# Loading the first row of wq in two halves, from two engines' DMA queues

## The chip, the cores and the metric

The kernel runs on one core of a Trainium2 chip. A core has five engines with an instruction stream each: TensorE (PE; PEld is its loading of weights), VectorE (DVE), ScalarE (ACT), GpSimd (POOL) and SyncE (SP, which here only issues DMAs). They are tied together by semaphores. Sixteen DMA engines move data between HBM and the core's memory of 128 partitions; SyncE and ScalarE each have a DMA queue that feeds them. The metric is device time in microseconds: the kernel before takes 99.17 us (median of three runs, 99.14 to 99.19).

## What is computed

One token passes through attention over a sliding window of a cached sequence and, in parallel, an MLP; both get the normalised input and their sum is added to x. All tensors are bf16.

```python
# x (1,1,1024), 32 query heads, 4 key/value heads, head size 128, window W = 4096 of Sk = 65536
xn = layernorm(x)
q = (xn @ wq).reshape(1, 1, 32, 128).transpose(0, 2, 1, 3)            # wq (1024, 4096)
k = repeat(k_cache[:, :, Sk - W:, :], 8, axis=1)                       # v alike
p = softmax(einsum("bhqd,bhkd->bhqk", q, k) * 128 ** -0.5)
attn = einsum("bhqk,bhkd->bhqd", p, v).transpose(0, 2, 1, 3).reshape(1, 1, 4096) @ wo
y = layernorm(xn)
mlp = gelu(y @ w1 + b1) @ w2 + b2                                      # w1 (1024, 3584)
return x + attn + mlp
```

With one token every weight is used once: 39.9 MB are read, and the arithmetic is matrix times vector.

## The kernel before

Nothing is tiled over the output; each weight matrix is loaded whole, in one or a few large DMAs, and its rows are spread over the partitions. For wq, partition p holds rows 8p to 8p+7, and "row r" of the loaded matrix below means the r-th of these eight in every partition (4096 bf16, 8 KB a partition, 1 MB in all). `WQ_CHUNKS = [1, 7]` loads row 0 by one DMA and rows 1 to 7 by a second, each with a semaphore of its own (`s_wq[0]`, `s_wq[1]`).

SyncE issues all the large loads in one order: wq's row 0, wq's rows 1 to 7 (57 KB a partition), then, after a wait for GpSimd's constants (L210), the K window, w1 and the V window; w2 once the product with wq is done (L323, for it overwrites wq); wo in chunks of 16, 8, 4 and 3 rows and two half rows, once the product with w1 is done (L422). ScalarE issues three small ones from its own queue: x (L191) and b1 (L192), which both come after a wait for two GpSimd memsets (L190, it counts POOL's `b1z`), and b2 (L246).

The work around these loads, in order: VectorE waits for x (`dve.wait_ge(s_x, 16)`, L241) and transposes it (L242); a chain of short instructions on VectorE, GpSimd, TensorE and ScalarE (L248 to L278) makes the two layer norms, `XNTb` for the attention and `YTb` for the MLP. TensorE multiplies `XNTb` with wq (`wide_product`, L306 to L319, recorded at L283): it waits for `s_wq[0]`, does the eight matmuls of row 0, waits for `s_wq[1]`, and does the 56 of rows 1 to 7. VectorE, ScalarE and TensorE bring q into the shape `QB` (L327 to L350). VectorE then waits for K and transposes it in place in four steps (L355); TensorE multiplies the scores behind each step; a softmax follows (L375 to L405). Then TensorE multiplies w1 (L411 to L418), p with V (L470 to L476), w2 (L516) and, chunk by chunk as it lands, wo (L545 to L551, after each chunk a few matmuls of `keep_busy` on no data of use). The last three rows of wo and the addition of the two half sums come at L556 to L583, and SyncE stores the result (L585).

On each engine the order is as written in the code; the wait that counts is a semaphore's value. A DMA adds 16 to its semaphore when it has landed:

```python
act.wait_ge(POOL.sem, C["b1z"])
act.dma_start(XB4[0:128:32, :], x_rows).then_inc(s_x, 16)
act.dma_start(B1R[0:128:32, :], b1_rows).then_inc(s_b1, 16)
```

Of the kernel before, what the change touches and what calls it, by code (L numbers as in the profile page):

```python
# [20 lines left out]
NQ = 4096  # L21
# [5 lines left out]
WQ_CHUNKS = [1, 7]  # L27
# [24 lines left out]
def bass_parallel_sum__sliding_block_cached__mixer_channel_mlp__decode_kernel(  # L52
# [18 lines left out]
    pe, dve, act, pool, sp = nc.tensor, nc.vector, nc.scalar, nc.gpsimd, nc.sync  # L71

    def sems(name, n):
        return [nc.alloc_semaphore(f"{name}{i}") for i in range(n)]

    s_x, s_b1, s_b2, s_out = (nc.alloc_semaphore(n) for n in ("s_x", "s_b1", "s_b2", "s_out"))
    s_wq = sems("s_wq", len(WQ_CHUNKS))
# [11 lines left out]
    def sb(name, shape, d):  # L89
        return nc.alloc_sbuf_tensor(name, shape, d)  # L90

    f32, bf16 = dt.float32, dt.bfloat16
    WA = sb("WA", [128, KC * NQ], bf16)
# [61 lines left out]
    wq_p = A_wq.rearrange("(p r) n -> p r n", r=KC)  # L155
# [8 lines left out]
    def load_rows(dst, src, chunks, width, semaphores, first=0, c0=0, off=0):  # L164
        for j, n in enumerate(chunks):
            sp.dma_start(  # L166
                dst[:, off + c0 * width: off + (c0 + n) * width].rearrange("p (c n) -> p c n", c=n),
                src[:, first + c0: first + c0 + n, :],
            ).then_inc(semaphores[j], 16)
            c0 += n  # L170
# [1 line left out]
    def load_cache(dst, src, sem):  # L172
        sp.dma_start(dst[:, :], src[0, :, SK - W:SK, :].rearrange("g (m b) d -> m g (b d)", m=32)).then_inc(sem, 16)

    load_rows(WA, wq_p, WQ_CHUNKS, NQ, s_wq)
    def d(ins):
        return DVE.mark(ins)

# [103 lines left out]
    def held(out, rhs, w, pos, size, start, stop, load=False):  # L282
        return pe.add_instruction(mybir.InstMatmult(  # L283
            name=nc.get_next_instruction_name(), engine=PEE, ldweights=load,
            start_tensor_calc=start, stop_tensor_calc=stop, tile_size=size, tile_position=pos,
            ins=[pe.lower_ap(rhs), pe.lower_ap(w, for_matmul_weights=True)], outs=[pe.lower_ap(out)]))
# [18 lines left out]

    def wide_product(weights, chunks, width, semaphores, vec, n, banks, name):  # L306
        for j, (k0, k1) in enumerate(chunks):
            pe.wait_ge(semaphores[j], 16)
            for k in range(k0, k1):
                w = vec[:, k:k + 1].to_broadcast([128, 32])  # L310
                for a in range(4):
                    pe.ldweights(w, tile_position=(0, 32 * a))  # L312
                for b in range(2):
                    for a in range(4):
                        lo = k * width + (2 * a + b) * n
                        last = held(PS[32 * a:32 * a + 32, banks[b] * 512: banks[b] * 512 + n], weights[:, lo:lo + n], w,
                                    (0, 32 * a), (128, 32), k == 0, k == KC - 1)
        C[name] = PE.mark(last)

    hinted = pe.mark_branch_hint_location()  # L320
    wide_product(WA, [(0, 1), (1, 8)], NQ, s_wq, XNTb, 512, [4, 5], "q")

    sp.wait_ge(PE.sem, C["q"])  # L323
# [293 lines left out]
```

## Time and profile before

| | |
|---|---|
| median of three runs | 99.17 us |
| the profiled execution | 99.34 us, of which 98.0 us are the span |
| busy: PE, DVE, ACT, POOL | 53.2, 41.8, 11.2, 8.2 us |
| read from HBM | 39.86 MB, 407 GB/s over the span |
| SyncE's queue, share of 16 DMA engines | 95.0% |
| wq row 0: issue to landing | 5.0 us |
| wq rows 1 to 7: issue to landing | 21.5 us |
| K: issue to landing | 25.9 us |

The span runs from the first to the last instruction of the execution that was profiled; the rest of its time lies around it. In the views, a line such as `22.72 5.80 PE L283 MATMUL ... [7.37 <-DMA WA<-in_A_wq_dram]` gives the start, the time to the end of the group, the engine, the line of the kernel, the operation with its tiles, and in brackets the idle time of that engine before it and what ended it. A tile is named without its number (KT is K's, later wo's; WA is wq's, later w2's; XB is x's). An engine's name with a q behind it (SPq, ACTq) is its sequencer issuing something. Windows give, for each stretch of time, the busy time of each engine with its number of instructions, the clock granted to TensorE, and the share and GB/s of the DMA engines; packets are counted in the stretch in which they start, so that short stretches can show more than 100%.

### The profile page before, as it was taken

The numbers are of one execution on the slowest core, as the hardware profiler recorded it, in microseconds if no ns is written. First come the engines' busy times: TensorE is split into PE (matmuls) and PEld (weight loads), VectorE is DVE, ScalarE is ACT, GpSimd is POOL, SyncE is SP. The second block draws the span as 40 slices with busy tenths as digits, with TensorE's granted clock in tenths as the row PEclk, the third lists the DMA queues.
The fourth block names the chain that finished last, engine by engine and source line by source line (L and its number), as shares of the span: only waits on it lengthen the run. The fifth ranks groups of instructions, "written<-read, shape, count | busy, mean of one in ns | idle before, by whom it ended". The sixth has DMA issues, their size and how long they took to land.

```text
span 98.0 us, 911 instructions
## 1 busy us (share of the span) xinstructions
PE 53.2 (54%) x376; PEld 13.4 (14%) x217; DVE 41.8 (43%) x45; ACT 11.2 (11%) x21; POOL 8.2 (8%) x33
## 2 busy tenths in 40 slices
PE   0000232007960947195361489878998677883781
PEld 0000220001100001011010111113332111220130
DVE  0000321000028899999999500987943400110042
ACT  0000527000022000000000489000000000000020
POOL 6776201000000000000000000000000000000000
PEclk9999999999999589957999755899999999999999
DMA  3999888999999988899599998889994999999960
GB/s 53 488 613 398 377 374 375 398 538 441 428 428 578 398 374 374 374 398 702 237 428 428 428 588 374 374 374 398 702 398 214 428 428 428 421 428 408 421 251 1
DMA packets 1765, 39.87 MB, mean 407 GB/s; under 512 B 216, under 2 KB 484, under 8 KB 612
## 3 DMA queue, kind: packets, MB, share of 16 engines
q1 hardware_dynamic: 1740, 39.85, 95.0%
q10 hardware_dynamic: 24, 0.01, 0.0%
q14 instruction: 1, 0.01, 0.0%
HBM read 39.86 MB, written 0.00 MB: 407 GB/s over the span
## 4 chain that ended last, share of the span: by engine, by line
DMA 52%; DVE 24%; PE 11%; POOL 5%; issue 3%; SPq 1%; ACT 1%; POOLq 0%; DVEq 0%
DMA KT<-in_A_k_cache_dram 26%; DMA KT<-in_A_wo_dram 26%; DVE KT L355 18%; PE PS L292 9%; DVE MX L375 2%; DVE MX L377 2%; POOL F L206 1%; POOL B1R L188 1%; SPq L166 1%; DVE KT L554 1%; DVE MR L388 1%; PE PS L559 1%; ACT Q L381 1%; POOL QB L198 1%; PE PS L283 1%
## 5 line engine op out<-in xcount | busy, mean ns | idle before, releaser
L355 DVE STREAM_TRANSPOSE KT<-KT 128x4096 bf16<-128x4096 bf16 x4 | 17.4, 4413 | 0.5 <-DMA KT<-in_A_k_cache_dram 0.5
L283 PE MATMUL PS<-KT,QB 128*128 128x512 bf16 x32 | 8.9, 427 | 7.6 <-DVE KT L355 7.6
L283 PE MATMUL PS<-WA,XNTb 128*32 128x512 bf16 x64 | 6.8, 605 | 7.4 <-DMA WA<-in_A_wq_dram 7.4
L292 PE MATMUL PS<-W,YTb 128*32 x64 | 8.2, 464 | 1.3 <-issue 0.9
L292 PE MATMUL PS<-V,WA 128*128 (+1 forms) x31 | 7.9, 381 | 0.5 <-issue 0.2
L292 PE MATMUL PS<-WA,GT 128*32 x56 | 6.7, 381 | 2.6 <-issue 1.8
L253 PE MATMUL PS<-XT,onesf 128*128 128x16 f32 x2 | 0.6, 385 | 10.9 <-POOL XT L251 10.9
L327 DVE CAST Q<-PS 128x512 bf16<-128x512 f32 x1 | 0.7, 691 | 12.6 <-PE PS L283 12.6
L242 DVE STREAM_TRANSPOSE XT<-XB 128x256 bf16<-128x256 bf16 x1 | 0.6, 625 | 9.7 <-DMA XB<-in_A_x_dram 9.7
L406 DVE STREAM_TRANSPOSE WA<-WA 128x4096 bf16<-128x4096 bf16 x1 | 4.4, 4436 | 0.0
L292 PE MATMUL PS<-W,OT 128*32 128x512 bf16 x48 | 2.9, 380 | 2.1 <-DMA W<-in_A_wo_dram 1.5
L367 PEld LDWEIGHTS <-QB 128*128 128x128 bf16 x16 | 1.7, 104 | 17.3 <-DVE KT L355 13.5
L554 DVE COPY KT<-PS 128x512 f32<-128x512 f32 x1 | 0.7, 692 | 7.6 <-PE PS L292 7.6
L520 DVE TENSOR_TENSOR OD<-PS,D 128x128 f32<-128x128 f32 x1 | 0.3, 292 | 8.4 <-PE PS L518 8.4
L292 PEld LDWEIGHTS PS<-V,WA 128*128 (+1 forms) x32 | 3.1, 96 | 4.7 <-issue 3.0
L283 PE MATMUL PS<-MRow,ML 128*128 128x512 bf16 x8 | 3.3, 581 | 0.7 <-DVE QB L348 0.7
L402 ACT ACTIVATE WA<-PS,NMB 128x1024 bf16<-128x1024 f32 (+1 forms) x2 | 3.1, 1536 | 1.2 <-DVE NMB L397 1.2
L381 ACT ACTIVATE Q<-PS 128x512 f32<-128x512 f32 x1 | 0.6, 597 | 22.5 <-DVE MX L377 22.5
L555 ACT ACTIVATE KT<-PS 128x512 f32<-128x512 f32 x1 | 0.6, 597 | 22.2 <-PE PS L292 22.2
L312 PEld LDWEIGHTS <-XNTb 128*32 128x32 bf16 x32 | 1.2, 138 | 12.1 <-DMA WA<-in_A_wq_dram 8.3
L292 PEld LDWEIGHTS PS<-W,YTb 128*32 x32 | 1.6, 98 | 7.5 <-issue 7.1
L257 ACT ACT_TABLE_LOAD x1 | 1.3, 1283 | 10.9 <-POOL XT L251 10.9
(105 smaller groups left out, 47.4 us busy)
## 6 DMA issues: line engine op xcount, KB each, us to landing
WA<-in_A_wq_dram SPq DMA_DIRECT2D x1, 7168.0 KB, 21.5
W<-in_B_w_dram SPq DMA_DIRECT2D x1, 7168.0 KB, 42.2
WA<-in_B_w_dram SPq DMA_DIRECT2D x1, 7168.0 KB, 47.4
KT<-in_A_k_cache_dram SPq DMA_DIRECT2D x1, 4096.0 KB, 25.9
V<-in_A_v_cache_dram SPq DMA_DIRECT2D x1, 4096.0 KB, 51.3
W<-in_A_wo_dram SPq DMA_DIRECT2D x1, 4096.0 KB, 18.9
W<-in_A_wo_dram SPq DMA_DIRECT2D x1, 2048.0 KB, 23.4
WA<-in_A_wq_dram SPq DMA_DIRECT2D x1, 1024.0 KB, 5.0
```

The lines of the kernel that those rows point to most:

```text
L257: C["std1"] = ACT.mark(act.activation(out=msx[:, 6:7], in_=msx[:, 5:6], func=ACTF.Sqrt, scale=-1.0, bias=EPSC[:, 0:1]))
L283: return pe.add_instruction(mybir.InstMatmult(name=nc.get_next_instruction_name(), engine=PEE, ldweights=load, start_tensor_calc=start, st ...
L292: return pe.add_instruction(mybir.InstMatmult(name=nc.get_next_instruction_name(), engine=PEE, ldweights=load, start_tensor_calc=start, st ...
L312: pe.ldweights(w, tile_position=(0, 32 * a))
L355: C["kt"].append(d(dve.transpose(KT[:, j * W:(j + 1) * W], KT[:, j * W:(j + 1) * W])))
L367: pe.ldweights(w, tile_position=(0, 0))
L375: d(dve.tensor_reduce(out=MX[:, 0:1], in_=PS[:, 0:2048], axis=AX.X, op=ALU.max))
L377: C["mx1"] = d(dve.tensor_reduce(out=MX[:, 1:2], in_=PS[:, 2048:4096], axis=AX.X, op=ALU.max))
L381: C["s7"] = ACT.mark(act.activation(out=S7, in_=bank(7), func=ACTF.Copy))
L402: C[f"exp{j}"] = C["exp"] = ACT.mark(act.activation(out=PT[:, lo:lo + n], in_=src, func=ACTF.Exp, bias=NMB[:, 0:1], scale=SCALE, accum_out ...
L406: C["PT"] = d(dve.transpose(PT, PT))
L554: C["S0"] = d(dve.tensor_copy(S[:, 0:DH2], bank(SB)))
```

## The change

Row 0 of wq is loaded by two DMAs of 64 partitions each, 0.5 MB apiece. SyncE issues the one for partitions 0 to 63, where it issued the whole row. ScalarE issues the one for partitions 64 to 127; it stands before every other instruction of ScalarE, and so before the wait at L190 and the loads of x and b1. Both add to `s_wq[0]`, and TensorE waits for 32 on it instead of 16. Rows 1 to 7 are loaded by SyncE as before, right after its half of row 0.

```diff
-    load_rows(WA, wq_p, WQ_CHUNKS, NQ, s_wq)
+    half_row = WQ_CHUNKS[0] * NQ
+    for eng, lo in ((sp, 0), (act, 64)):
+        eng.dma_start(WA[lo:lo + 64, 0:half_row], wq_p[lo:lo + 64, 0, :]).then_inc(s_wq[0], 16)
+    load_rows(WA, wq_p, WQ_CHUNKS[1:], NQ, s_wq[1:], first=WQ_CHUNKS[0], off=WQ_CHUNKS[0] * NQ)
     def d(ins):
         return DVE.mark(ins)
...
     def wide_product(weights, chunks, width, semaphores, vec, n, banks, name):
         for j, (k0, k1) in enumerate(chunks):
-            pe.wait_ge(semaphores[j], 16)
+            pe.wait_ge(semaphores[j], 16 if j else 32)
             for k in range(k0, k1):
```

## The prediction

> **What bounds the kernel now.** I read the chain of work that ended last first, then the order of time up to the first use of K, then fine windows of the loads, then the end of TensorE's order of time. All times are of one profiled execution: span 98.0 us, 99.34 us with the 1.34 us around it. That is 0.17 us above the median of the runs shown, 99.17, so a sum made on it loses 0.17 at the end.
>
> ```profile
> DMA 52%; DVE 24%; PE 11%; POOL 5%; issue 3%; SPq 1%; ACT 1%; POOLq 0%; DVEq 0%
> DMA KT<-in_A_k_cache_dram 26%; DMA KT<-in_A_wo_dram 26%; DVE KT L355 18%; PE PS L292 9%; DVE MX L375 2%; DVE MX L377 2%; POOL F L206 1%; POOL B1R L188 1%; SPq L166 1%; DVE KT L554 1%; DVE MR L388 1%; PE PS L559 1%; ACT Q L381 1%; POOL QB L198 1%; PE PS L283 1%
> ```
>
> Two loads make half of the chain: K, and the last rows of wo. Both are the tail of one stream, so the question is whether that stream ever pauses. In these windows the last two columns are the busy share of the 16 DMA engines and GB/s, and a packet counts where it starts:
>
> ```profile
> 6.80:7.00 0.20, 0.00 (x0) 0.00 (x0) 0.00 (x0) 0.00 (x0) 0.17 (x1) 1.00 2.66 1152
> 7.00:7.20 0.20, 0.00 (x0) 0.00 (x0) 0.00 (x0) 0.00 (x0) 0.20 (x1) 1.00 6.64 2872
> 7.20:7.40 0.20, 0.00 (x0) 0.00 (x0) 0.00 (x0) 0.00 (x0) 0.14 (x2) 1.00 0.66 287
> ...
> 9.20:9.40 0.20, 0.00 (x0) 0.00 (x0) 0.00 (x0) 0.00 (x0) 0.12 (x2) 1.00 3.97 1720
> 9.40:9.60 0.20, 0.00 (x0) 0.00 (x0) 0.00 (x0) 0.00 (x0) 0.16 (x1) 1.00 0.00 0
> 9.60:9.80 0.20, 0.00 (x0) 0.00 (x0) 0.14 (x1) 0.00 (x0) 0.00 (x0) 1.00 0.66 287
> ```
>
> 287 GB/s over 0.2 us is 57 KB: one packet, the seven rows of wq that one partition gets (7 x 8 KB). Its share, 0.66 of 16 engines over 0.2 us, is 2.11 us of one engine. So each engine starts such a packet every 2.11 us, with no gap, and one engine starts each round on its own, some 0.3 us after the rest (9.60; by the packet records 0.27 behind the next and 0.47 behind the middle one). It has that lag from its first packet of the first row (8 KB, 1126 ns; a later 8 KB packet takes 309 ns) and keeps it to the end: its first-row mark is at 5.38 us, that of the last load at 95.19. The loads are a rigid block; its start, and the latest engine in it, set the last landing.
>
> The second question is how the two DMA queues share an engine (packets, MB, share; first from 2.00 to 6.85 us, then 6.85 to 7.20):
>
> ```profile
> q1 hardware_dynamic: 150, 1.88, 93.8%
> ...
> q1 hardware_dynamic: 14, 0.80, 529.5%
> q10 hardware_dynamic: 4, 0.00, 1.9%
> ```
>
> q1 is SyncE's, q10 ScalarE's. ScalarE's load of x (4 rows of 512 B, one to an engine) is issued from 1.98 to 3.05, yet no packet of it runs before 6.85. It starts at 6.91 to 7.13, when its four engines have ended their first 57 KB packet; its completion mark comes one more such packet later, at 9.05 to 9.27; b1 one more later, at 11.17. So in this stretch the engine alternates: one packet of q1, one of q10, and each packet of q10, even a mark, costs 2.11 us.
>
> The order of time shows what waits for x:
>
> ```profile
> 0.74 0.86 SPq L166 DMA_DIRECT2D WA<-in_A_wq_dram  x2
> 1.98 1.07 ACTq L191 DMA_DIRECT2D XB<-in_A_x_dram  x1
> 9.66 0.62 DVE L242 STREAM_TRANSPOSE XT<-XB 128x256 bf16<-128x256 bf16 x1 [9.66 <-DMA XB<-in_A_x_dram]
> 14.31 1.03 PE L283 MATMUL PS<-WA,XNTb 128*32 128x512 bf16 x8
> 22.72 5.80 PE L283 MATMUL PS<-WA,XNTb 128*32 128x512 bf16 x56 [7.37 <-DMA WA<-in_A_wq_dram]
> 31.34 0.59 DVE L348 CAST QB<-PS 32x128 bf16<-32x128 f32 x2 [0.33 <-PE PS L339]
> 32.39 17.42 DVE L355 STREAM_TRANSPOSE KT<-KT 128x4096 bf16<-128x4096 bf16 x4 [0.45 <-DMA KT<-in_A_k_cache_dram]
> ```
>
> The first row's eight matmuls end at 15.34, and TensorE then waits 7.37 us for the other seven rows. Behind that, VectorE waits 0.45 us for K. So x may be 7.37 + 0.45 = 7.82 us late before the work from 32.39 on moves. The last reserve is at the end:
>
> ```profile
> 88.02 1.12 PE L298 MATMUL PS<-identf 128*128 128x512 f32 x2
> 90.63 1.04 PE L292 MATMUL PS<-W,OT 128*32 128x512 bf16 x16 [1.49 <-DMA W<-in_A_wo_dram]
> 91.60 0.81 PE L298 MATMUL PS<-identf 128*128 128x320 f32 x2
> 93.12 0.60 PE L292 MATMUL PS<-KT,OT 128*32 128x512 bf16 x8 [0.71 <-DMA KT<-in_A_wo_dram]
> ```
>
> TensorE waits 1.49 us for wo's second chunk and 0.71 us for the third: 2.20 us more.
>
> **The change, part by part.** *Issue on SyncE.* Its first DMA shrinks from 128 rows to 64; two issues stay (0.86 us for both), so the seven-row load is issued no later. Its packets can be there about 1.0 us after an issue starts (0.74 to the first packet at 1.75), by 2.7 at worst; an engine needs at least 3 x 0.31 us after its first packet's end (2.55 to 3.24) for its half of the row. No gap, price 0.
>
> *Issue on ScalarE.* One DMA more ahead of x's. SyncE's first issue took about 0.4 us, ScalarE's first 1.07. From 0.7 it ends at 1.1 to 1.8, before ScalarE's wait on GpSimd's memset is over (1.96), so x is issued when it was. If x's 1.07 was a first-use cost, it moves to the new DMA. Price on the sequencer 0. The b2 load and the rest of ScalarE's work come behind x in any case.
>
> *The stream.* The bytes of each engine stay: 4 + 4 packets of 8 KB in place of 8, and one mark more (9 ns). Changing queue costs nothing visible: an engine ends a 57 KB packet, runs x's in 27 ns, and starts the next at once. Price of the stream 0.01 us, if the half loads run at 309 ns a packet; the bounds are below.
>
> *TensorE's wait* asks for 32 in place of 16: the same wait on both halves. Behind it on TensorE stands the whole of q; ScalarE and VectorE wait for q at 28.57, SyncE too, to issue w2, whose turn comes only after v (landed at 59).
>
> *The queue that x is moved back in.* This is the step with a price. Ahead of x, in q10, each engine now has four 8 KB packets and a mark. SyncE's ring holds only four such packets before the 57 KB ones, so it is past them at 3.5 to 3.8 on x's engines. Packets of q10 that run while SyncE's 8 KB ones do are free; each that comes later costs one 57 KB packet. How many is not shown; the bounds are two rounds ahead of x's mark, as now (x at 9.66), and eight. The nearest row is x itself: queued 1.0 us before SyncE's last 8 KB packets ended at 4.8 if its delay is like that of SyncE's first load, it was still passed over until a 57 KB packet had run. If ScalarE's half does as x did, it misses SyncE's 8 KB packets and one 57 KB packet: 57 KB packets then stand ahead of its four packets, its mark, x and x's mark, seven. I take seven. x's mark then comes at 3.65 + 7 x 2.11 + 4 x 0.31 = 19.7 in place of 9.2, 10.5 us late. Then: 10.5 - 7.37 (wait for the seven rows) = 3.1 late for q; - 0.45 (wait for K) = 2.7 late from 32.39 on. From there to 88 I find no wait that absorbs it: VectorE, TensorE and ScalarE hand over within 0.1 us, and wo's issue, now at 69.5, is still before w2's last packets end at 75.5. - 1.49 = 1.2 late at wo's second chunk, - 0.71 = 0.5 at the third. The first row itself has landed by then (its last packets at about 13 and mark at 15).
>
> *Sum:* 0 + 0 + 0.01 + 0.47 = 0.5 us: 99.34 + 0.5 = 99.8, less 0.17: 99.65. With six rounds x is 8.4 late, 0.6 after VectorE's wait, and the 1.49 hides it: 99.2. With eight it is 12.6 late and 2.6 at the end: 101.7.
>
> **The rivals.** *Hidden.* The halves alternate from the start, or six rounds at most: x is late, nothing else is. For it: 10.0 us of reserve in all. Against it: x's own six microseconds of waiting. 99.2.
>
> *Faster: the start.* The end hangs on one engine's first packet (1126 ns, the others 307 to 1024). SyncE's loop reaches its 16 engines from 1.75 to 2.32; with half the rows it may reach the late ones sooner, and a second queue may fill a slow engine's start. It decides if that engine's lag goes and x is under 10 us late: 0.27 if only the next one is left (98.9), 0.47 if all are as the middle one (98.7). Against it: first packets end at 2.55 or later however early they start, and the same rows are read cold.
>
> *Slower: the half loads at half rate.* Every wide packet here runs at 26.5 to 27 GB/s, whatever its size, and no row tells whether the engine or the 128 partitions written set that. If it is the partitions, 16 engines on 64 of them take 618 ns a packet. Full price 7 x 0.31 = 2.2 us, none if the two halves always run against each other; the middle is 1.1: 100.3. Against it, weakly: b1's four packets (1792 B, 74 ns) were written while the other twelve engines poured 57 KB packets into the same memory, and none of those took over 2.12 us.
> [...]
>
> **How the numbers follow.** x behind the 57 KB packets 0.40 (of which eight rounds 0.07), hidden 0.25, faster start 0.20, half rate 0.15. The likeliest gives 99.65; its own range is 99.4 to 99.9 (the latest engine's lag moved by 0.25). From 98.85 to 100.9 leaves out some 0.05 below and 0.11 above. 0.2% (0.2 us) is about what can be told from no change. Faster 0.20, same 0.25, slower 0.55.
>
> **What would show it.** Right: VectorE's first transpose at about 20, the first row's product at 24 to 25 with no wait for the seven rows behind it, VectorE's work on K starting at 35 with no wait for K (which lands at 32.4 as before), and TensorE's two waits for wo gone. Hidden: the transpose before 18.5. Faster: no lone packet 0.3 us behind each round, and K landing before 32.2. Half rate: share and GB/s near half between 2.6 and 5 us, and K landing after 33. I am wrong above all if ScalarE's first packets reach the engines by 2.5 and take turns with SyncE's small ones.

## The result, and the profile after

The changed kernel takes 101.86 us (median of 7 runs) against 99.18 for the kernel before (7 runs beside it): a ratio of 1.0282, 95% interval 1.0262 to 1.0302, or 2.68 us slower. The forecast was slower, but 99.65, and the time lies outside the range of 98.85 to 100.9. The profiled execution has a span of 100.6 us; its own time, 102.91, has 2.3 us around the span where six others have 1.3 to 1.4, so I compare spans and medians, not that number.

The chain of waits is what it was, with the K load longer:

```profile
DMA 53%; DVE 24%; PE 11%; POOL 5%; issue 3%; SPq 1%; ACT 1%; POOLq 0%; DVEq 0%
DMA KT<-in_A_k_cache_dram 28%; DMA KT<-in_A_wo_dram 25%; DVE KT L358 17%; PE PS L295 9%; DVE MX L378 2%; DVE MX L380 2%; POOL F L209 1%; POOL B1R L191 1%; SPq L166 1%; DVE KT L557 1%; DVE MR L391 1%; PE PS L562 1%; ACT Q L384 1%; POOL QB L201 1%; DVE ORow L585 1%
```

In the order of time everything from x on is 2.5 to 2.9 us later, 2.6 at the rows shown here, and the waits in them are within 0.2 us of what they were (before: 9.66, 14.31, 22.72 after a wait of 7.37, and 32.39 after one of 0.45):

```profile
0.73 0.57 ACTq L177 DMA_DIRECT2D WA<-in_A_wq_dram  x1
0.74 0.59 SPq L177 DMA_DIRECT2D WA<-in_A_wq_dram  x1
1.39 0.81 SPq L166 DMA_DIRECT2D WA<-in_A_wq_dram  x1
...
12.29 0.63 DVE L245 STREAM_TRANSPOSE XT<-XB 128x256 bf16<-128x256 bf16 x1 [12.29 <-DMA XB<-in_A_x_dram]
16.94 1.04 PE L286 MATMUL PS<-WA,XNTb 128*32 128x512 bf16 x8
25.34 5.67 PE L286 MATMUL PS<-WA,XNTb 128*32 128x512 bf16 x56 [7.36 <-DMA WA<-in_A_wq_dram]
...
35.02 4.45 DVE L358 STREAM_TRANSPOSE KT<-KT 128x4096 bf16<-128x4096 bf16 x1 [0.61 <-DMA KT<-in_A_k_cache_dram]
```

TensorE's waits for wo at the end are unchanged too, 1.48 and 0.73 us (before 1.49 and 0.71):

```profile
93.25 1.04 PE L295 MATMUL PS<-W,OT 128*32 128x512 bf16 x16 [1.48 <-DMA W<-in_A_wo_dram]
...
95.75 0.60 PE L295 MATMUL PS<-KT,OT 128*32 128x512 bf16 x8 [0.73 <-DMA KT<-in_A_wo_dram]
```

So no engine is late by itself: the stream of loads is late as a block. Where it lost the time shows in the windows of row 0 (last two columns: busy share of the 16 DMA engines, GB/s by the packets that start there), of the kernel before and of the changed one:

```profile
3.50:4.50 1.00, 0.00 (x0) 0.00 (x0) 0.00 (x0) 0.00 (x0) 0.82 (x3) 1.00 1.06 451
```

```profile
3.50:4.50 1.00, 0.00 (x0) 0.00 (x0) 0.00 (x0) 0.00 (x0) 0.82 (x3) 1.00 1.10 246
4.50:5.50 1.00, 0.00 (x0) 0.00 (x0) 0.00 (x0) 0.00 (x0) 0.79 (x3) 1.00 1.09 254
5.50:6.50 1.00, 0.00 (x0) 0.00 (x0) 0.00 (x0) 0.00 (x0) 0.71 (x5) 1.00 1.02 213
```

The engines are as busy as before (1.02 to 1.10, before 1.06) and move about half as much (213 to 254 GB/s, before 451): by the records of single packets, one of 8 KB takes about 0.61 us in place of 0.31. And the two halves do not share the time. From 2.00 to 4.20 us only ScalarE's queue (q10) has packets; from 4.20 to 6.55 SyncE's (q1) has its 61, beside what is left of the other (windows of the DMA queues: packets, MB, share):

```profile
q10 hardware_dynamic: 61, 0.50, 103.5%
...
q1 hardware_dynamic: 61, 0.50, 95.9%
q10 hardware_dynamic: 19, 0.02, 5.8%
```

By the packet records the first packet starts at 2.09 us (before 1.75), row 0's last mark is at 7.53 (5.38), and the seven rows' last mark at 24.76 (22.30). The first 57 KB packet of each engine is slow too, 2.40 to 2.89 us in place of 2.12, and the 2.40 is that of the latest engine, which starts when no packet of the halves is left; why is open. From there on the block is 2.5 us late to its end (last mark 97.73; before 95.19).

### The profile page after: what moved, and what is told of

The parts are those of the page before. It is cut to its first block, busy times and chain, and to the rows that moved or that the text cites. A ratio compares the mean times of both kernels' runs of the same rounds, so it can differ in the third digit from the quotient of the medians.

```text
span 100.6 us, 912 instructions
## 1 busy us (share of the span) xinstructions
PE 53.3 (53%) x376; PEld 13.3 (13%) x217; DVE 41.8 (42%) x45; ACT 11.2 (11%) x21; POOL 8.2 (8%) x33
## 4 chain that ended last, share of the span: by engine, by line
DMA 53%; DVE 24%; PE 11%; POOL 5%; issue 3%; SPq 1%; ACT 1%; POOLq 0%; DVEq 0%
DMA KT<-in_A_k_cache_dram 28%; DMA KT<-in_A_wo_dram 25%; DVE KT L358 17%; PE PS L295 9%; DVE MX L378 2%; DVE MX L380 2%; POOL F L209 1%; POOL B1R L191 1%; SPq L166 1%; DVE KT L557 1%; DVE MR L391 1%; PE PS L562 1%; ACT Q L384 1%; POOL QB L201 1%; DVE ORow L585 1%
```

## The experiments

Three theories stood against each other for the half rate. D: a load into 64 partitions gets half the rate, whoever issues it; in its count form the rate goes with the number of partitions. Q: two queues filled at once slow each other. R: it is the reading of 64 rows of HBM that is slow. The later start and the forecast's own mechanism, x queued behind row 0, were tried apart from it. All runs are timed against runs of the kernel before on the same chip.

### Both halves from SyncE

```diff
-    for eng, lo in ((sp, 0), (act, 64)):
+    for eng, lo in ((sp, 0), (sp, 64)):
```

> Both half loads are issued by SyncE, one after the other, then the seven rows; ScalarE's queue is as in the kernel before. Theory D (a load into 64 partitions gets half the rate, whoever issues it): both halves still run at about 225 GB/s, one after the other, for some 4.5 us; the seven rows and K land 2.1 to 2.4 us later than before (K at 34.5 to 34.8), time 101.3 to 101.6. Theory Q (two DMA queues filled at once slow each other): one queue alone, so row 0 runs at about 425 GB/s, K lands at 32.4 and the time is 99.2. The first packet starts at 1.75 as before if the 0.34 us later start of the changed kernel came from two engines issuing at once, and at 2.1 if it came from the shape of the load.

101.83 us against 99.21, ratio 1.0256 (1.0226 to 1.0286). K's transposes start at 34.89. One queue alone has the whole loss, so Q falls. The first packet starts at 2.12: two engines issuing at once are not what starts it later. And x plays no part: its transpose starts at 8.04, 4.25 us earlier than in the change, and the time is the same.

```profile
3.50:4.50 1.00, 0.00 (x0) 0.00 (x0) 0.00 (x0) 0.00 (x0) 0.83 (x3) 1.00 1.11 229
```

### Two queues, halves by columns

```diff
-    for eng, lo in ((sp, 0), (act, 64)):
-        eng.dma_start(WA[lo:lo + 64, 0:half_row], wq_p[lo:lo + 64, 0, :]).then_inc(s_wq[0], 16)
+    for eng, lo in ((sp, 0), (act, half_row // 2)):
+        eng.dma_start(WA[:, lo:lo + half_row // 2], wq_p[:, 0, lo:lo + half_row // 2]).then_inc(s_wq[0], 16)
```

> Two loads from two queues as in the change, but each takes half of the columns of row 0 (4 KB) into all 128 partitions. Theory D: packets at the full rate (about 155 ns for 4 KB); what is left is the later start, so K lands at 32.4 to 32.8 and the time is 99.2 to 99.6. Theory Q: as the change, 101.5 to 101.9, K at 35.

99.39 us against 99.21, ratio 1.0027 (1.0004 to 1.0051), with the span of before, 98.0. K's transposes start at 32.42 (before 32.39), and the first packet at 1.74. By the profiles two queues at once cost the stream nothing here: the last mark is at 95.19 with and without them. The 0.2 us of the medians are too few for two profiles to place (the spans of the runs have medians of 98.05 and 97.9), and I leave them open.

```profile
3.50:4.50 1.00, 0.00 (x0) 0.00 (x0) 0.00 (x0) 0.00 (x0) 0.81 (x3) 1.00 1.00 414
```

### The same reads, into all partitions

```diff
-        eng.dma_start(WA[lo:lo + 64, 0:half_row], wq_p[lo:lo + 64, 0, :]).then_inc(s_wq[0], 16)
+    for eng, h in ((sp, 0), (act, 1)):
+        eng.dma_start(WA[:, h * half_row // 2:(h + 1) * half_row // 2],
+                      wq_p[64 * h:64 * h + 64, 0, :].rearrange("p (b n) -> p b n", b=2)).then_inc(s_wq[0], 16)
```

> Two loads from two queues that read the very rows of HBM that the change's halves read (partitions 0 to 63 of the matrix by SyncE, 64 to 127 by ScalarE), but write them into 128 partitions of 4 KB each. Row 0 of wq is therefore misplaced and the result is not the reference's; no instruction's time depends on it. Theory D: full rate, 99.2 to 99.6, K at 32.4 to 32.8. Theory R (the reads of 64 rows, 64 KB apart, are what is slow): 101.4 to 101.9, K at 34.5 to 35. Theory Q: the same as R.

99.72 us against 99.21, ratio 1.0061 (1.0027 to 1.0095). The rows of HBM that the change reads come at 418 GB/s when they go into 128 partitions (246 in the change, 451 before), so R falls. The first packet starts at 2.20 and K's transposes at 32.66: what is lost goes with the start.

```profile
3.50:4.50 1.00, 0.00 (x0) 0.00 (x0) 0.00 (x0) 0.00 (x0) 0.83 (x3) 1.00 1.02 418
```

### Every other partition

```diff
-    for eng, lo in ((sp, 0), (act, 64)):
-        eng.dma_start(WA[lo:lo + 64, 0:half_row], wq_p[lo:lo + 64, 0, :]).then_inc(s_wq[0], 16)
+    for eng, odd in ((sp, 0), (act, 1)):
+        eng.dma_start(WA[odd:128:2, 0:half_row], wq_p[odd:128:2, 0, :]).then_inc(s_wq[0], 16)
```

> The change with the halves dealt out differently: SyncE loads the even partitions, ScalarE the odd ones, 64 partitions each, 8 KB apiece, two queues. [...] Count form: 101.4 to 101.9.

99.59 us against 99.15, ratio 1.0044 (1.0030 to 1.0058). Same engines, same queues, same number of partitions and bytes as the change, and 2.2 us less: the steady packets take 309 ns. So here it is not how many partitions a load has but which; why, the traces do not show. The remaining 0.44 us goes with the start: SyncE's issue takes 0.57 us (0.38 to 0.41 for wq's two loads in the kernel before), the first packet starts at 2.08, and the seven rows' last mark, at 22.55, is 0.25 us later than in the profile of before.

```profile
3.50:4.50 1.00, 0.00 (x0) 0.00 (x0) 0.00 (x0) 0.00 (x0) 0.82 (x3) 1.00 0.96 401
```

### Four loads of 32 partitions

```diff
-    for eng, lo in ((sp, 0), (act, 64)):
-        eng.dma_start(WA[lo:lo + 64, 0:half_row], wq_p[lo:lo + 64, 0, :]).then_inc(s_wq[0], 16)
+    for lo in range(0, 128, 32):
+        sp.dma_start(WA[lo:lo + 32, 0:half_row], wq_p[lo:lo + 32, 0, :]).then_inc(s_wq[0], 16)
```

TensorE waits for 64 on the semaphore.

> Row 0 by four loads of 32 partitions each, all from SyncE, in order. [...] Count: the rate goes with the number of partitions, a quarter of the full rate for 32: packets of about 1.2 us, row 0 takes 9 to 10 us, time 106 to 107.

101.22 us against 99.15, ratio 1.0200 (1.0183 to 1.0217). The steady packets take about 0.6 us, as with 64 partitions, not 1.2: the form by count falls. It is 0.6 us faster than the two halves from SyncE; 0.35 us of that is the first packet, which starts at 1.77 again, and the rest I can't place. So the later start belongs to loads of 64 rows here, not to all loads under 128; why, these runs do not show.

```profile
3.50:4.50 1.00, 0.00 (x0) 0.00 (x0) 0.00 (x0) 0.00 (x0) 0.82 (x3) 1.00 0.89 197
4.50:5.50 1.00, 0.00 (x0) 0.00 (x0) 0.00 (x0) 0.00 (x0) 0.79 (x3) 1.00 1.04 238
```

### Twice the dose

Rows 0 and 1 by halves (`WQ_CHUNKS = [2, 6]`), all else as in the change.

> The change with twice the dose: rows 0 and 1 by two loads of 64 partitions (16 KB a partition), rows 2 to 7 by the third. If the loss is the half rate, it grows with the bytes: 2 x 2.4 us at half rate + 0.35 us of later start less what the first packets hide, K at 37.1 to 37.6, time 104.0 to 104.6. If the loss is a cost of each load (a start, a mark, a change of queue), it stays at 101.8.

104.73 us against 99.15, ratio 1.0588 (1.0528 to 1.0649): 5.58 us for two rows, 2.68 for one. The loss goes with the bytes, as D has it; the second row costs 2.90 us. K's transposes start at 37.84, and like the time this is a little past the bracket. A 16 KB packet takes 1.26 us at the median of SyncE's half, where wo's of that size take 0.61.

### ScalarE's half issued late

The change, with ScalarE's half moved behind the wait for GpSimd's memset, just ahead of x:

```diff
-    for eng, lo in ((sp, 0), (act, 64)):
-        eng.dma_start(WA[lo:lo + 64, 0:half_row], wq_p[lo:lo + 64, 0, :]).then_inc(s_wq[0], 16)
+    sp.dma_start(WA[0:64, 0:half_row], wq_p[0:64, 0, :]).then_inc(s_wq[0], 16)
...
         act.wait_ge(POOL.sem, C["b1z"])
+        act.dma_start(WA[64:128, 0:half_row], wq_p[64:128, 0, :]).then_inc(s_wq[0], 16)
         act.dma_start(XB4[0:128:32, :], x_rows).then_inc(s_x, 16)
```

> The change with ScalarE's half issued where x's load was, behind the wait for GpSimd's memset, at about 2.0 us, and x behind it. If the step of the prediction holds that ScalarE's packets, once SyncE's small ones are past, run one to each 57 KB packet, then x lands at 17 to 20 us in place of 12.3, TensorE waits for x and not for the seven rows, and the time is above what the half rate alone gives. Theory D for the rate: SyncE's half alone is slow (4 packets of 0.6 us), ScalarE's packets meet 57 KB packets of all partitions and slow half of the engines by 0.3 us for each, in all 1.2 to 2.5 us: 100.4 to 101.7 if x stays hidden, up to 103 if it does not. If instead ScalarE's half again runs whole, before SyncE's next packet, x lands by 14 and the time is 101.3 to 101.9.

104.36 us against 99.21, ratio 1.0477 (1.0404 to 1.0550), more than any of the expectations. x's transpose starts at 26.90 and TensorE has all 64 matmuls with no wait between:

```profile
26.90 0.62 DVE L245 STREAM_TRANSPOSE XT<-XB 128x256 bf16<-128x256 bf16 x1 [26.90 <-DMA XB<-in_A_x_dram]
...
31.55 5.51 PE L286 MATMUL PS<-WA,XNTb 128*32 128x512 bf16 x64
```

The packets of the two queues do alternate now (from 6 to 16 us 48 of SyncE's queue and 47 of ScalarE's), and in the rounds where a half packet meets the 57 KB packets of all partitions both are slow: one pair of packets takes about 3.1 us (2.5 to 3.0 for the 57 KB one, mostly 0.3 to 0.6 for the 8 KB one) against 2.11 + 0.31 = 2.42 without a conflict. The next kernel differs from this one in nothing but which partitions the halves hold, and its last mark is 4.54 us earlier (95.67 against 100.21): 0.73 of this stands at the end of SyncE's half, and 3.7 more at the end of the seven rows. That is more than a fair sharing of one 8 KB packet (0.31 us a round) would cost; why is open. The profile is of the longest of this kernel's four runs (span 103.1 us, the others 101.9 to 102.6).

### The same, every other partition

The forecast's own mechanism without the half rate: SyncE's half is `WA[0:128:2]`, ScalarE's late half `WA[1:128:2]`.

> The prediction's own mechanism without the half rate: SyncE loads the even partitions of row 0 as its first DMA, ScalarE the odd ones from where x's load was (about 2.0 us), x behind. Packets at the full rate (309 ns). If the recorded step holds, ScalarE's packets come one to each 57 KB packet: seven rounds ahead of x's mark, x at 20 to 20.5 us, TensorE's wait for the seven rows gone, K's transposes at about 35 with no wait for K, TensorE's 1.49 us and most of its 0.71 us for wo gone, time 99.6 to 100.1, of which 0.2 to 0.35 is the later start of a load of 64 rows. If an engine needs eight rounds, x at 22.5 and 101.5 to 102. If ScalarE's half runs whole, as in the change: x at 10 to 12 and 99.6.

99.88 us against 99.19, ratio 1.0066 (1.0049 to 1.0082). By the packet records nearly every engine runs its four small packets of SyncE's, and then 57 KB, 8 KB, 57 KB, 8 KB and so on (from 6 to 16 us 74 packets of SyncE's queue and 72 of ScalarE's): seven 57 KB packets ahead of x's mark, which comes at 20.01 to 20.22.

```profile
20.60 0.62 DVE L245 STREAM_TRANSPOSE XT<-XB 128x256 bf16<-128x256 bf16 x1 [20.60 <-DMA XB<-in_A_x_dram]
25.26 5.97 PE L286 MATMUL PS<-WA,XNTb 128*32 128x512 bf16 x64
...
34.73 4.45 DVE L358 STREAM_TRANSPOSE KT<-KT 128x4096 bf16<-128x4096 bf16 x1
```

VectorE waits for no K, as forecast, but TensorE still waits 1.35 and 0.72 us for wo at the end, so the queue, which exists as I described it, is hidden there. The 0.69 us go with the last landing, whose mark is 0.49 us later than in the profile of before. The first packet starts at 2.10, and one engine's first packet takes 1.43 us (at most 1.04 with every other partition and both loads early), so I take this for the start once more; no run shows it apart.

### No load of its own for row 0

`WQ_CHUNKS = [8]` in the kernel before: one load, one wait.

> The other direction from the kernel before: no row 0 of its own, all eight rows of wq by one load from SyncE, and one wait in the product. The stream has the same bytes and one mark less: last landing within 0.1 us of before, unless the first packets, now 64 KB, change the latest engine's lag of 0.5 us. TensorE has all 64 matmuls behind the landing of wq: q 0.9 to 1.0 us later, VectorE 0.5 us later at K, which the 1.49 us before wo's second chunk hides. Time 99.0 to 99.3. If the prediction's reserve at wo does not exist, 99.7.

99.46 us against 99.15, ratio 1.0038 (1.0015 to 1.0061); the profiled execution has the span of before, 98.0, with K's transposes at 32.37. q is not 1 us later, as I had expected: the 64 matmuls end at 28.48 where the 56 ended at 28.52. But the time is above the 99.0 to 99.3 of the expectation, and the 0.3 us are in the spans of the runs (median 98.1, of the kernel before 97.8). The two profiles can't place them, for that of before is of a long execution and this one of a short one. So the separate row 0 may be worth 0.3 us; by what, is open.

## Why the prediction was wrong, point by point

Set by the mark of the last landing, the runs lie on one line: the time is that mark and 4.0 to 4.3 us. The marks are of one profiled execution each, the times are medians; the profile of before, of 99.34 us, is some 0.2 us above its median, so differences of marks come out by about that much too small.

| kernel | last mark, us | time, us | over before |
|---|---|---|---|
| before | 95.19 | 99.18 | |
| columns | 95.19 | 99.39 | 0.18 |
| one load | 95.24 | 99.46 | 0.31 |
| every other partition | 95.42 | 99.59 | 0.44 |
| same reads | 95.43 | 99.72 | 0.51 |
| every other, late | 95.67 | 99.88 | 0.69 |
| four of 32 | 97.15 | 101.22 | 2.07 |
| both from SyncE | 97.67 | 101.83 | 2.62 |
| the change | 97.73 | 101.86 | 2.68 |
| halves, late | 100.21 | 104.36 | 5.15 |
| two rows | 100.62 | 104.73 | 5.58 |

*The stream as a rigid block that sets the end: right.* Every load after wq kept its distance to within 0.2 us, and the end followed the last landing in all eleven kernels.

*"Price of the stream 0.01 us, if the half loads run at 309 ns a packet": this is the step that failed.* They run at about 0.61. The case was on the list with the price of 2.2 us at most, and the two kernels that differ in nothing but the choice of the 64 partitions give 2.68 - 0.44 = 2.24 us for it. I gave it 0.15 and took the middle, 1.1, for the trace of before has no load of 64 partitions and could not tell whether the halves run one after the other; they do (q10 to 4.20, q1 after), so the price is the upper end. No run has the two halves work against each other, so that they would then cost nothing is not shown. Nor is the whole price in row 0, where I reckoned it: from the first packet to the row's last mark is 5.44 us in place of 3.63, 1.8 us more, and another 0.3 comes from the latest engine's first 57 KB packet. That the sum meets the upper end is in part luck. The sign that I named was half right: GB/s fell to about half (246 for 451), the engines' share did not fall (1.10 for 1.06).

The row that I read against it, b1's packets of 74 ns beside 57 KB packets of 2.12 us, proves nothing about loads that all 16 engines write into one half at once. What the runs show of the choice of partitions: blocks of 64 neighbours ran at 246 GB/s against 451 from 3.50 to 4.50 us; a packet of 8 KB took about 0.6 us in blocks of 64 and of 32 alike; and two loads of every other partition, 64 each, ran at 309 ns a packet, as the whole row did. By which mechanism is not shown.

*"Issue on SyncE ... price 0": wrong by 0.2 to 0.4 us.* The half's issue takes 0.59 us, more than the whole row's 0.38, and the stream starts 0.34 us later. The later start moved the whole block (with every other partition the seven rows' last mark by 0.25 us and the last of all by 0.23); I had asked only whether a gap opens behind it. What it comes to is seen best in the kernel with every other partition, at most 0.44 us.

*"ScalarE's half does as x did": wrong.* x was issued at 1.98, 0.8 us after SyncE's second load; the half is issued at 0.73, with SyncE's first, and its four packets and mark ran before SyncE's half. My sign of being wrong came true in part: ScalarE's first packets were there by 2.5, at 2.09, but they took no turns with SyncE's. Two rounds of 57 KB packets stand ahead of x's mark, as before, and x is 2.6 us late with everything else. When the half is issued at 1.98, the seven rounds come as worked out (x's mark at 19.7 forecast, 20.0 to 20.2 measured).

*The reserves behind x: too small.* With x's transpose 10.9 us late, K's transposes were 2.3 late (2.7 forecast), but wo's first matmuls only 0.7 (86.90 for 86.19). The wait that I said was not there is TensorE's before the product with w2:

```profile
75.05 0.60 PE L292 MATMUL PS<-ZERO,SELQ 128*128 128x512 bf16 x2
76.44 0.94 PE L292 MATMUL PS<-WA,GT 128*32 x8 [0.80 <-DVE HW L482]
77.72 0.94 PE L292 MATMUL PS<-WA,GT 128*32 x8 [0.34 <-issue]
```

```profile
77.37 0.60 PE L295 MATMUL PS<-ZERO,SELQ 128*128 128x512 bf16 x2
77.90 1.35 PE L295 MATMUL PS<-WA,GT 128*32 x14
```

Before (first fence) TensorE idles 0.80 us there. The profile puts it down to VectorE's L482, but the code waits there for w2, and w2 lands at 75.96, 47.4 us after its issue at 28.56; the loop's first matmul follows 0.5 us behind. In the late kernel (second fence) that wait is gone, and the first matmuls of the loop follow each other without the pauses of before: 0.86 and 0.73 us of reserve that I had not counted. So even seven rounds would not have made the 0.5 us of the forecast. The sign of the forecast was right for a reason that played no part.

## What to carry to other kernels

Before a load is cut by partitions, ask which partitions each piece writes while all the DMA engines work on it. Here the rate nearly stayed when the load was cut by columns or the partitions were dealt out alternately (414 and 401 GB/s from 3.50 to 4.50 us, 451 before), and about halved when the load was cut into blocks of 64 or 32 neighbouring partitions (246 and 197). In this kernel, whose loads never pause, what slowed and delayed the first load was paid in full at the end (the change's seven rows and its last landing are 2.46 and 2.54 us later than before), while a wait in the middle had reserves behind it: where x's transpose was 10.9 us late, with every other partition and ScalarE's half late, the whole cost 0.69 us. A small load in a second queue beside large packets paid one large packet, 2.12 us, for each of its packets and marks here, if it came after the large ones were queued; ScalarE's half, issued before them, paid none.

## What was not expected of the hardware

As the first load of its queue, issued at 0.73 or 0.74, a load into 64 partitions took 0.57 to 0.59 us to issue, and the first packet started at 2.08 to 2.12, about 0.35 us later than with a load into 128 in the kernel before and in the cut by columns (0.38 to 0.41 us; 1.74 to 1.75). 64 rows read into 128 partitions took 0.65 to 0.66 us and started at 2.20; four loads into 32 partitions took 1.78 us together and started at 1.77. Two loads issued at the same time from two queues, at 0.73 and 0.74, ran one almost whole before the other in the change, 61 of ScalarE's 64 packets ahead of SyncE's first; what decides that is not shown. And a packet into one half of the partitions that met a 57 KB packet of all partitions cost the pair 0.7 us, about twice its own 0.31.
